# HGRN2 attention and a multiplicative FFN on one core: two early chunks in the later form, a fixed early order on VectorE, and a check in place of a clamp

## The chip, the core and the metric

One core of a Trainium2 chip runs the whole program: TensorE (PE) multiplies, VectorE (DVE), ScalarE (ACT) and GpSimd (POOL) do the elementwise work, and SyncE (SP) issues all the loads and stores as DMAs. Each engine takes its own list of instructions in order and waits on semaphores for the others. The metric is the device time of one execution in microseconds; lower is better. The time before is the median of 3 runs.

## What is computed

```
# attention: B,H,S,D = 4,8,768,48, all float32
f = 1 / (1 + exp(-f_logit))
for t in range(S):
    state = f[t][:, None] * state + outer(k[t], v[t])      # per batch and head, 48x48
    y[t] = q[t] @ state
x = y.transpose(0, 2, 1, 3).reshape(B * S, H * D)          # 3072 x 384
# FFN: w1, w2 384x1024; w3 1024x1024; w_out 1024x384, all float64
out = ((x @ w1) * (x @ w2)) @ w3 @ w_out                   # 3072 x 384, float32
```

## The kernel before

**Chunks.** The sequence is cut into 24 chunks of 128 steps (`NU`, six per batch). In a chunk the four pairs of heads lie side by side in 512 columns, two heads on partitions 0 to 47 and 64 to 111. ScalarE makes the gates by a sigmoid (L380); VectorE runs a forward scan over them (L388), a reciprocal (L398), a backward scan (L410), and multiplies to K (L418) and Q (L404). TensorE turns K (L455), forms K against Q, ScalarE copies the result (A), GpSimd cuts it to the causal half (L571), TensorE multiplies with v and adds what the state gives, and VectorE carries the state on.

**Two forms.** Chunks 0 to 3 (`u < NPE`) go in the *early form*: whole 128x128 products of K and Q (`pairs`, L431), `first_values` (L469, L475), `first_update` (L487), the state on VectorE (L687 to L690), and x^T by TensorE: `moved` multiplies with a permutation (L739), `settled` copies it into `xt` (L744). Chunks 4 to 23 go in the *later form*: 64-row tiles that run beside each other (L441, L548, L515, L534), a state in the middle of the chunk (`middle`, L619 to L624), a later gain (L683), and x^T by memory: `written` stores to DRAM (L731, two DMAs), `gathered` loads it back transposed (L734).

**FFN.** Four chunks make a block of 512 tokens, six blocks in all. Block 0 and a part of block 1 go by `part`: for each slice `jc` of 128 of the 1024 columns a product with w1, copied by ScalarE (L798), a product with w2, and VectorE's multiplication of the two (L803); block 0 takes the first four slices for two chunks at a time, the last four for all four. All other blocks go by seven products in place of eight (`seven`: TensorE L761, ScalarE's copies L864 and L892, VectorE L885 to L903), fed by sums of x^T (L831) and of the weights (L1253). w3 and w_out are folded into one matrix first: eight folds (L1221), copied by ScalarE (L1228), with sums of it (L1267). The down products use it (L997 to L1053). At most four banks of accumulators, the pool `f`, are open at once.

**Weights.** They arrive as float64, each number as two 32-bit words. `fetch` loads a piece (L1138), and each piece is made float32 by five instructions: ScalarE takes the magnitude of the high words (`magnitude`, L1157) and prepares the low words (`rest`, L1160); VectorE clamps the magnitude into the range whose exponent can be moved (L1163), shifts it by three bits (L1164), joins sign and low bits (`signed`, L1168) and adds (`joined`, L1174). There are 12 pieces of w1 and w2 (128x512), 4 of w_out (128x768) and 8 of w3 (128x1024). The landing buffers lie in one tile, `place`; a load waits until the piece that was there before is signed.

**Order.** `Plan` holds every step as a task with an engine, a cost in us, what it waits for, and a priority. `order()` takes again and again the task that can start first, lowest priority value among equals, and emits the instructions in that order; DMA slots (`lane`, 8), banks (`f`) and buffers (`ab`) are part of it. `need(u)` and the due times in `weights()` set the priorities. Until 35 us of planned time (`FULL`), holes in TensorE's list are filled with products of a constant (L268).

**The end.** `judge` looks at the ranges of the gates' products, `told` and `heard` send its result through DRAM, and before the last product of the last block (`final`, L1045) all engines read it: outside the safe range a general version of the attention runs instead of accepting the result.

Of the kernel before, what the change touches and what calls it, by code (L numbers as in the profile page):

```python
# [60 lines left out]
NPE = 4  # L61
# [7 lines left out]
W = C // 2  # L69
FULL = 35.0  # L70
FLOOR = 2.0**-60
# [3 lines left out]
class Plan:  # L75
# [16 lines left out]
    def add(self, eng, cost, emit, deps=(), prio=0.0, takes=(), frees=(), lag=0.2, slack=0.0):  # L92


        t = {
            "eng": eng, "cost": cost, "emit": emit, "deps": [d for d in deps if d is not None], "prio": prio,
            "takes": list(takes), "frees": list(frees), "lag": lag, "slack": slack, "at": None, "end": None, "no": len(self.tasks),
        }
        self.tasks.append(t)
        return t  # L100

    def order(self):
        free, done, left = {}, [], list(self.tasks)
        enders = {}
        for t in self.tasks:
            for f in t["frees"]:
                enders.setdefault(id(f), []).append(t)

        def after(t, ds):

            if any(d["end"] is None for d in ds):
                return None
            return max([0.0] + [d["end"] + (d["lag"] + t["slack"] if d["eng"] != t["eng"] else 0.0) for d in ds])

        def places(t, name):

            ends = [(after(t, enders[id(h)]) if h else 0.0, i) for i, h in enumerate(self.pools[name])]
            return [e for e in ends if e[0] is not None]

        def start(t):  # L120

            waits, at = list(t["deps"]), free.get(t["eng"], 0.0)
            for name in t["takes"]:
                if name in self.pools:
                    ends = places(t, name)
                    if not ends:
                        return None
                    at = max(at, min(ends)[0])
                    continue
                n, taken = self.slots[name]  # L130
                if len(taken) >= n:
                    waits += enders[id(taken[-n])]
            ready = after(t, waits)
            return None if ready is None else max(at, ready)

        while left:
            at, _, _, t = min(
                ((at, t["prio"], t["no"], t) for t in left if (at := start(t)) is not None), key=lambda x: x[:3]
            )
            t["at"], t["end"] = at, at + t["cost"]  # L140
            free[t["eng"]] = t["end"]
            for name in t["takes"]:
                if name in self.pools:
                    t["got"] = min(places(t, name))[1]
                    self.pools[name][t["got"]] = t
                else:
                    self.slots[name][1].append(t)
            left.remove(t)
            done.append(t)
        return sorted(done, key=lambda t: (t["at"], t["no"]))  # L150
# [3 lines left out]
def kernel(  # L154
# [19 lines left out]
    with tc.manual_schedule():  # L174
        outside = ranged(tc, q, k, f_logit, v, w1, w2, w3, w_out, out, ident, w12, wc, left)
        with tc.If(outside > 0, preferred_fallthrough_block=True, label="general"):
            general(tc, q, k, f_logit, v, leaf_mask, out, ident, w12, wc)
# [17 lines left out]
def ranged(ctx, tc, q, k, f_logit, v, w1, w2, w3, w_out, out, ident, w12, wc, left):  # L195
# [17 lines left out]
    back = keep.tile([R, NQ], F32, name="back")  # L213
    gate = [keep.tile([R, NQ + 1], F32, name=f"gate{i}") for i in range(2)]
    qs, ks, fs = ([keep.tile([R, NQ], F32, name=f"{nm}{i}") for i in range(n)] for nm, n in (("q", 3), ("k", 2), ("f", 2)))
    masked = [keep.tile([P, 2, HP, C], F32, name=f"A{i}") for i in range(2)]
    flat = [t.rearrange("p r h c -> p (r h c)") for t in masked]
# [105 lines left out]
    def need(u):  # L323
        return (0.0, 1.0, 2.0, 3.0)[u] if u < 4 else 60 + 14.5 * (u - 4)
# [4 lines left out]
    def moves(n, size, rate, emit, deps, prio, late=0.0):  # L329


        for j in range(n):
            i = plan.add("SP", 0.45, (lambda: None) if j else emit, [d] if j else deps, prio - j * 1e-3, takes=["lane"], lag=0.6)
            d = i
            t = plan.add("DMA", size / n / rate, lambda: None, [i], prio - j * 1e-3, lag=1.3 + late, frees=[i])
# [6 lines left out]
    def front(u):  # L342

        s, t = st[u], tk[u]
        n0 = need(u)

# [18 lines left out]

        t["lf"] = moves(2, 197, 250, load(fu, f_logit), free(2, "g"), n0 - 30)
        t["lk"] = moves(2, 197, 250, load(ku, k), free(2, "k"), n0 - 29.5)
        t["lq"] = moves(2, 197, 250, load(qu, q), free(3, "q"), n0 - 29)

        def load_v():  # L370
# [5 lines left out]
            n0 - (28.2, 28.2, 28.2, 29.6, 12)[min(u, NPE)],  # L376
# [29 lines left out]
        t["q"] = plan.add("DVE", 0.7, scale_q, [t["p"], t["lq"]] + past(u, 3, "v", "a"), n0 + 0.1)  # L406
# [13 lines left out]
        t["k"] = plan.add("DVE", 0.7, scale_k, [t["r"], t["lk"]] + past(u, 2, "a", "t"), n0)  # L420
# [209 lines left out]
    def rest(u):  # L630
# [13 lines left out]
        else:  # L644
            middle(u)
            more = u + 1 < NU
            after = tk[u + 1] if more else {}

            def visit():
# [4 lines left out]
                else:  # L654
                    s["pa"] = ps.tile([P, 2, NQ], F32, name="pa")
                    nc.tensor.transpose(out=s["pa"][:, 0, 0:R], in_=s["K"][:, 0:C], identity=ident[0:R, 0:R])
# [93 lines left out]
        else:  # L750
            t["z"] = moves(2, 197, 250, written, [t["y"]], n0 - 100)
            t["x"] = moves(1, 197, 250, gathered, [t["z"]] + before, n0 - 100)
# [13 lines left out]
    def ffn(n):  # L766
# [188 lines left out]
        if n == 0:  # L955
            part(0, 2, range(KH))
            part(2, 4, range(KH))
            part(0, 4, range(KH, KF))
# [150 lines left out]
    def fetch(loads_, a, prio, subs, deps=()):  # L1109
# [30 lines left out]
        ld = moves(1, total, 380, load, held, prio, max(0.0, 3.5 - 1.2 * load_no) if load_no < 4 * KM else 3.0)  # L1140
# [5 lines left out]
        def sub(c0, c1, dst, due, waits):  # L1146
# [9 lines left out]
            def magnitude():  # L1156
                nc.scalar.activation(m, hi.bitcast(F32), AF.Abs)  # L1157

# [3 lines left out]
            def shifted():  # L1162
                nc.vector.tensor_scalar(m, m, HIGH, LOW, ALU.min, ALU.max)  # L1163
                nc.vector.tensor_scalar(m.bitcast(U32), m.bitcast(U32), 3, None, ALU.logical_shift_left)  # L1164
# [12 lines left out]
            b = plan.add("ACT", 0.2 + 0.43 * w, magnitude, [ld] + past, due)  # L1177
            e = plan.add("ACT", 0.2 + 0.43 * w, rest, [ld], due)
            h = plan.add("DVE", 0.32 + 0.54 * w, shifted, [b], due)
            g = plan.add("DVE", 0.16 + 0.53 * w, signed, [e, b] + list(waits), due)  # L1180
# [13 lines left out]
    def weights():  # L1194
        due = {(0, 0): 5.0, (1, 0): 8.0, (0, 1): 24.0, (1, 1): 26.0}
        pieces.update({key: [] for key in due})
        for half in range(2):
            for which, w in enumerate((w1, w2)):
                for kc in range(KM):
# [3 lines left out]
                        [(slice(0, P), src)], 1, -26 + 9.5 * half + 0.5 * which + 0.1 * kc,  # L1203
                        [(0, KH * P, w12_part(which, kc, c0), due[which, half] + 0.1 * kc, [])],
                    )

        done = []
# [67 lines left out]

    def judge():
# [7 lines left out]
        good = work.tile([R, 1], F32, name="good")  # L1284
        nc.vector.tensor_scalar(low, low, RANGE, None, ALU.is_ge)
        nc.vector.tensor_tensor(good, low, nil, ALU.mult)
        where["good"] = good

    def told():
        where["all"] = dram.tile([R, 1], F32, name="good")  # L1290
        nc.sync.dma_start(where["all"], where["good"])

    def heard():
        row = work.tile([1, R], F32, name="row")
# [9 lines left out]
    for u in range(NU):  # L1304
        if u <= NPE:
            front(u)
        if u == NPE:
            turning(u)
            begin(u)
        if u >= NPE and u + 1 < NU:  # L1310
# [3 lines left out]
        if u == NPE - 1:  # L1314
            weights()
        if u == NU - 1:
            looked = plan.add("DVE", 1.0, judge, [tk[i]["y"] for i in range(NU)], -20)
            sent = moves(1, 0.4, 250, told, [looked], 0, 20.0)
            judged = plan.add("DVE", 0.2, decided, [moves(1, 0.4, 250, heard, [sent], 0, 20.0)], -20)
        if u % UB == UB - 1:  # L1320
            ffn(u // UB)
    ready_at = 0.0
# [8 lines left out]
    return blk[NB - 1]["outside"]  # L1331

# [336 lines left out]
```

## Time and profile before

| what | value |
|---|---|
| time, median of 3 runs | 477.67 us (477.29 to 477.99) |
| the profiled execution | 482.72 us, its span 481.0 us, mean granted TensorE clock 0.995 |
| VectorE / ScalarE / GpSimd busy | 362.8 us (75%) / 141.1 us (29%) / 62.5 us (13%) |
| bytes read / written | 40.67 MB / 8.65 MB |
| L388 and L410, the scans, 24 each | 29.6 us and 30.0 us |
| L418, L404: K and Q of a chunk, 112x512 | 738 ns, 684 ns |
| L1163 / L1164, 128x512, 12 each | 418 ns / 427 ns |
| L1168 / L1174, 128x512 pieces, 12 each | 758 ns / 690 ns |
| L1157 / L1160, 128x512, 12 each | 682 ns / 692 ns |
| load of a weight piece, 512 KB / 768 KB / 1024 KB, issue to landing | 9.7 us / 6.9 us / 4.7 us |
| yt<-ys / xt<-yt, issue to landing | 2.4 us / 2.9 us |

The span is that of one profiled execution, from the first to the last instruction; it took about 5 us more than the median of the runs. Lines such as L1163 are those of the kernel printed above. A duration in the profile includes an overlap with the next instruction of the same engine, so that the distance from start to start, which the timeline shows, is shorter.

### The profile page before, as it was taken

The numbers are of one execution on the slowest core, as the hardware profiler recorded it, in microseconds if no ns is written. First come the engines' busy times: TensorE is split into PE (matmuls) and PEld (weight loads), VectorE is DVE, ScalarE is ACT, GpSimd is POOL, SyncE is SP. The second block draws the span as 40 slices with busy tenths as digits, with TensorE's granted clock in tenths as the row PEclk, the third lists the DMA queues.
The fourth block names the chain that finished last, engine by engine and source line by source line (L and its number), as shares of the span: only waits on it lengthen the run. The fifth ranks groups of instructions, "written<-read, shape, count | busy, mean of one in ns | idle before, by whom it ended". The sixth has DMA issues, their size and how long they took to land.

```text
span 481.0 us, 11341 instructions
## 1 busy us (share of the span) xinstructions
PE 468.7 (97%) x4667; PEld 400.4 (83%) x4667; DVE 362.8 (75%) x706; ACT 141.1 (29%) x310; POOL 62.5 (13%) x88
## 2 busy tenths in 40 slices
PE   8899999999999899999999999999999999999996
PEld 7788644656799688889988889988899888889995
DVE  7999699999999689899999567357653667664541
ACT  4697456462313334432432110001100110110000
POOL 9300000013303133312422100000000000000000
PEclk9999999999999899999999999999999999999999
DMA  6899277743415566446531002000111000000011
GB/s 183 269 387 236 54 278 246 260 138 100 134 50 162 163 172 169 115 132 169 148 110 46 18 18 65 34 33 2 34 33 58 9 0 1 0 1 1 34 66 37
DMA packets 36618, 50.10 MB, mean 104 GB/s; under 512 B 4546, under 2 KB 26050, under 8 KB 35538
## 3 DMA queue, kind: packets, MB, share of 16 engines
q1 hardware_dynamic: 36562, 49.33, 33.6%
q8 instruction: 37, 0.61, 0.6%
q14 instruction: 19, 0.16, 0.1%
HBM read 40.67 MB, written 8.65 MB: 103 GB/s over the span
## 4 chain that ended last, share of the span: by engine, by line
PE 73%; DVE 13%; DMA 6%; POOL 3%; issue 2%; ACT 1%; SPq 1%; DVEq 0%; POOLq 0%; ACTq 0%
PE f L761 62%; DVE place L1168 2%; PE f L1221 2%; DMA place<-in_w_dram 2%; PE py L515 2%; DVE place L1174 2%; DMA place<-in_w_out_dram 2%; PE f L455 2%; PE pa L441 2%; PE pa L548 2%; PE py L534 1%; DMA f<-in_f_logit_dram 1%; SPq L1138 1%; POOL ab L306 1%; DVE place L1253 1%
## 5 line engine op out<-in xcount | busy, mean ns | idle before, releaser
L761 PE MATMUL f<-xt,w 128*128 128x256 f32 (+1 forms) x600 | 162.8, 401 | 3.2 <-ACT gate L380 2.0
L761 PEld LDWEIGHTS f<-xt,w 128*128 128x128 f32 x600 | 114.1, 192 | 29.5 <-issue 10.0
L761 PE MATMUL f<-place 128*128 128x192 f32 (+1 forms) x504 | 112.1, 349 | 0.1
L761 PEld LDWEIGHTS f<-place 128*128 128x128 f32 x504 | 87.7, 190 | 6.2 <-DVE place L1010 0.4
L571 POOL TENSOR_SCALAR_AFFINE_SELECT A<-A 64x512 f32<-64x512 f32 (+1 forms) x44 | 40.7, 925 | 120.3 <-ACT A L565 110.5
L1221 PE MATMUL f<-place 128*128 128x384 f32 x128 | 42.8, 489 | 0.2 <-DVE place L1174 0.2
L864 ACT COPY a<-f 128x256 f32<-128x256 f32 x36 | 13.4, 373 | 93.2 <-PE f L761 78.0
L1221 PEld LDWEIGHTS f<-place 128*128 128x128 f32 x128 | 23.8, 190 | 16.5 <-DVE place L1174 0.8
L761 PE MATMUL f<-xt,place 128*128 128x256 f32 x144 | 37.3, 382 | 0.0
L761 PE MATMUL f<-wc,ab 128*128 128x192 f32 x192 | 35.2, 327 | 0.0
L761 PEld LDWEIGHTS f<-wc,ab 128*128 128x128 f32 x192 | 32.0, 190 | 0.5
L410 DVE TENSOR_TENSOR_SCAN bwd<-gate,back 112x512 f32<-112x512 f32 x24 | 30.0, 1249 | 0.8
L388 DVE TENSOR_TENSOR_SCAN fwd<-gate,floor 112x512 f32<-112x512 f32 x24 | 29.6, 1233 | 1.1 <-ACT gate L380 0.3
L761 PEld LDWEIGHTS f<-xt,place 128*128 128x128 f32 x144 | 26.6, 189 | 3.3
L888 DVE TENSOR_TENSOR place<-f,a 128x256 f32<-128x256 f32 x36 | 15.3, 424 | 18.6 <-PE f L761 18.4
L1157 ACT ACTIVATE place<-place 128x512 f32<-128x512 f32 (+2 forms) x24 | 21.3, 886 | 8.2 <-DVE w L1174 3.8
L1160 ACT ACTIVATE place<-place 128x512 f32<-128x512 uint32 (+2 forms) x24 | 21.1, 885 | 5.1 <-DMA place<-in_w_out_dram 5.1
L674 POOL TENSOR_TENSOR G<-lasts,gate 112x4 f32<-112x4 f32 x20 | 11.1, 556 | 87.3 <-ACT lasts L393 55.2
L710 ACT ACTIVATE ys<-py 112x512 f32<-112x512 f32 x20 | 11.9, 596 | 35.6 <-PE py L534 34.6
L761 PE MATMUL f<-place,w 128*128 128x256 f32 x72 | 21.4, 379 | 0.0
L899 DVE TENSOR_TENSOR ab<-f,place 128x256 f32<-128x256 f32 x36 | 15.2, 423 | 6.2 <-PE f L761 5.3
L997 DVE TENSOR_TENSOR place<-ab 128x512 f32<-128x512 f32 x24 | 16.9, 702 | 3.5 <-PE f L761 3.5
(126 smaller groups left out, 642.9 us busy)
## 6 DMA issues: line engine op xcount, KB each, us to landing
place<-in_w_dram SPq DMA_DIRECT2D x8, 1024.0 KB, 4.7
place<-in_w_dram SPq DMA_DIRECT2D x12, 512.0 KB, 9.7
out_dram<-o SPq DMA_DIRECT2D x24, 192.0 KB, 1.9
q<-in_q_dram SPq DMA_DIRECT2D x46, 96.0 KB, 2.8
vt<-in_v_dram SPq DMA_DIRECT2D x23, 192.0 KB, 3.4
k<-in_k_dram SPq DMA_DIRECT2D x44, 96.0 KB, 2.3
f<-in_f_logit_dram SPq DMA_DIRECT2D x43, 96.0 KB, 2.5
yt<-ys SPq DMA_DIRECT2D x40, 96.0 KB, 2.4
```

What stands on the lines that cost most here:

```text
L388: nc.vector.tensor_tensor_scan(s["P"], gate[u % 2][:, 0:NQ], floor, 0.0, ALU.mult, ALU.max)
L410: nc.vector.tensor_tensor_scan(s["R"][:, ::-1], gate[u % 2][:, NQ:0:-1], back[:, ::-1], 0.0, ALU.mult, ALU.max)
L571: nc.gpsimd.affine_select(out=a, in_=a, pattern=pattern, compare_op=ALU.is_ge, fill=0.0, base=0, channel_multiplier=-1,)
L710: nc.scalar.activation(ys, py, AF.Copy, accum_out=ysum[:, u : u + 1])
L761: nc.tensor.matmul(out_, lhsT=lhs[i], rhs=rhs[i], start=start and i == 0, stop=i == len(lhs) - 1, skip_group_check=True,)
L864: nc.scalar.copy(q["a"], q["X"])
L888: nc.vector.tensor_tensor(ups["u3", k], q["Y"], q["a"], ALU.add)
L899: nc.vector.tensor_tensor(m if which else to(tok, half), q[bank_], m, ALU.add)
L997: nc.vector.tensor_tensor(abs_[j], x, y, op)
L1157: nc.scalar.activation(m, hi.bitcast(F32), AF.Abs)
L1160: nc.scalar.activation(lo.bitcast(F32), lo, AF.Copy, bias=2.0, scale=2.0**-51)
L1221: nc.tensor.matmul(w3s["p", jc], lhsT=w3s[jc][:, kc * P : kc * P + P], rhs=wos[:, kc], start=(kc == 0), stop=(kc == KF - 1),)
```

## The change

- **Forms.** `NPE` goes from 4 to 2: chunks 2 and 3 take the later form, x^T by memory included. They are not interleaved with the next chunk's products as later chunks are: a second constant, `SOLO`, keeps that for chunk 4 on.
- **VectorE's early order.** The string `EARLY` names the items in the order in which VectorE takes them after chunks 0 and 1: A, the first half of w1's columns; chunks 2 and 3; B, the first half of w2; C and D, the second halves of w1 and w2. Each item's first step waits for the last steps of the one before. The loads are asked for in the same order.
- **No clamp.** `magnitude` and the clamp go; the shift reads the high words directly, every second word of the landed piece, and drops the sign by itself.
- **A check.** `ranges` loads all weights once more after the last chunk, in 34 pieces of 512 numbers a partition, into the two buffers of A, and has ScalarE sum magnitudes (`AF.Abs`) and signs against a small bias (`AF.Sign`) of the high words; VectorE's `verdict` turns the sums into a yes or no that joins `judge`'s. For weights outside the range, `convert` makes them again with the clamp before the general version runs.
- **The plan's costs.** Every engine starts at 0.6; DMA rates and lags differ, transfers cost more in two stretches (`CROWDED`), DMA tasks queue by the time of their issue, and some loads have an earliest time (`since`, `AHEAD`).
- **Block 0** takes its last four slices in two halves of two chunks, like the first four. The last chunk's extra transpose (L656) goes.

```diff
-NPE = 4
+NPE = 2
+SOLO = 4
+WIDE = 2 * HP * C
+LOOK = WIDE // 2
+BEGIN = 0.6
+SURE = 2.0
+SURE_X = 1.0
+SURE_W = 2.0
+DUE = (5.0, 8.0, 24.0, 26.0)
+EARLY = "A23BCD"
+CROWDED = [(13.5, 19.5, 1.6), (33.0, 46.0, 1.3)]
+AHEAD = 22.0
...
-            t["at"], t["end"] = at, at + t["cost"]
+            t["at"], t["end"] = at, at + t["cost"] * slower(t, at)
...
         with tc.If(outside > 0, preferred_fallthrough_block=True, label="general"):
+            if w1.dtype != F32:
+                convert(tc, w1, w2, w3, w_out, w12, wc)
             general(tc, q, k, f_logit, v, leaf_mask, out, ident, w12, wc)
...
-    masked = [keep.tile([P, 2, HP, C], F32, name=f"A{i}") for i in range(2)]
-    flat = [t.rearrange("p r h c -> p (r h c)") for t in masked]
+    both = keep.tile([P, 2 * WIDE], F32, name="A")
+    flat = [both[:, i * WIDE : i * WIDE + WIDE] for i in range(2)]
+    masked = [t.rearrange("p (r h c) -> p r h c", r=2, h=HP) for t in flat]
...
-            more = u + 1 < NU
+            more = u + 1 < NU and u >= SOLO
...
-            part(0, 4, range(KH, KF))
+            part(0, 2, range(KH, KF))
+            part(2, 4, range(KH, KF))
...
-            def magnitude():
-                nc.scalar.activation(m, hi.bitcast(F32), AF.Abs)
-
             def rest():
                 nc.scalar.activation(lo.bitcast(F32), lo, AF.Copy, bias=2.0, scale=2.0**-51)
 
             def shifted():
-                nc.vector.tensor_scalar(m, m, HIGH, LOW, ALU.min, ALU.max)
-                nc.vector.tensor_scalar(m.bitcast(U32), m.bitcast(U32), 3, None, ALU.logical_shift_left)
+                nc.vector.tensor_scalar(m.bitcast(U32), hi, 3, None, ALU.logical_shift_left)
...
-            b = plan.add("ACT", 0.2 + 0.43 * w, magnitude, [ld] + past, due)
             e = plan.add("ACT", 0.2 + 0.43 * w, rest, [ld], due)
-            h = plan.add("DVE", 0.32 + 0.54 * w, shifted, [b], due)
-            g = plan.add("DVE", 0.16 + 0.53 * w, signed, [e, b] + list(waits), due)
+            h = plan.add("DVE", 0.16 + 0.27 * w, shifted, [ld] + past, due)
+            g = plan.add("DVE", 0.16 + 0.53 * w, signed, [e, h] + list(waits), due)
...
+    def ranges():
+
+        seen = [w[kc * P : kc * P + P] for w in (w1, w2) for kc in range(KM)] + [w3[jc] for jc in range(KF)]
+        seen.append(w_out.rearrange("(p a) c -> p (a c)", a=KF))
+        seen = [w[:, c : c + LOOK] for w in seen for c in range(0, w.shape[1], LOOK)]
+        n = len(seen)
+        sums_, counts, small = (spare[:, a : a + m] for a, m in ((0, n), (64, n), (128, 1)))
...
+        def load(i):
+            return lambda: nc.sync.dma_start(words[:, i % 2 * WIDE : (i % 2 + 1) * WIDE], seen[i].bitcast(U32))
+
+        def total(i):
+            a = hi[:, i % 2 * LOOK : (i % 2 + 1) * LOOK]
+            return lambda: nc.scalar.activation(a, a, AF.Abs, accum_out=sums_[:, i : i + 1])
+
+        def count(i):
+            a = hi[:, i % 2 * LOOK : (i % 2 + 1) * LOOK]
+            return lambda: nc.scalar.activation(a, a, AF.Sign, bias=small, accum_out=counts[:, i : i + 1])
+
+        for i in range(n):
+            ld = moves(1, LOOK, 400, load(i), last[:1] if i < 2 else last[i - 1 : i], 500 + i, SURE_W)
+            a = plan.add("ACT", 0.92, total(i), [ld], 500 + i)
+            last.append(plan.add("ACT", 0.95, count(i), [a], 500 + i))
+
+        def verdict():
+            nc.vector.tensor_scalar(sums_, sums_, LARGE, None, ALU.is_le)
+            nc.vector.tensor_scalar(counts, counts, LOOK - 0.5, None, ALU.is_ge)
+            nc.vector.tensor_tensor(sums_, sums_, counts, ALU.mult)
+            where["weights"] = small
+            nc.vector.tensor_reduce(out=small, in_=sums_, axis=AX.X, op=ALU.min)
+
+        return plan.add("DVE", 0.5, verdict, last, -20)
...
+    for item in EARLY:
+        if item in "ABCD":
+            half, which = divmod("ABCD".index(item), 2)
+            mine = pieces[which, half]
+            first[item], last[item] = [j["deps"][0] for j in mine], mine
+        else:
+            t = tk[int(item)]
+            first[item], last[item] = [t["p"]], [t["q"], t["k"]]
+    for a, b in zip("1" + EARLY, EARLY):
+        for t in first[b]:
+            t["deps"] += last[a] if a != "1" else [tk[1]["q"], tk[1]["k"]]
```

`convert`, which runs only where the general version does:

```
def convert(ctx, tc, w1, w2, w3, w_out, w12, wc):
...
    def single(src, dst):
...
        nc.scalar.activation(m, hi.bitcast(F32), AF.Abs)
        nc.scalar.activation(lo.bitcast(F32), lo, AF.Copy, bias=2.0, scale=2.0**-51)
        nc.vector.tensor_scalar(m, m, HIGH, LOW, ALU.min, ALU.max)
        nc.vector.tensor_scalar(m.bitcast(U32), m.bitcast(U32), 3, None, ALU.logical_shift_left)
...
```

## The prediction

> **What bounds the kernel now.** I read the page's busy shares and chain first, then the timelines of the engines where TensorE stops, then the windows there.
>
> ```profile
> PE 468.7 (97%) x4667; PEld 400.4 (83%) x4667; DVE 362.8 (75%) x706; ACT 141.1 (29%) x310; POOL 62.5 (13%) x88
> ...
> PE 73%; DVE 13%; DMA 6%; POOL 3%; issue 2%; ACT 1%; SPq 1%; DVEq 0%; POOLq 0%; ACTq 0%
> ```
>
> TensorE is busy for 97% of the span. Its last matmuls start at 474.75 us and take 1.46; 4.8 us of copy and store follow. So the end moves only by what TensorE idles, or by what it gets done before it is full. The chain puts 13% on VectorE, but where VectorE is fullest TensorE was full as well:
>
> ```profile
> 34.74 15.71 PE L761 MATMUL f<-xt,w 128*128 128x256 f32 x72
> 51.64 26.05 PE L761 MATMUL f<-xt,w 128*128 128x256 f32 x72 [1.20 <-ACT ab L798]
> 77.53 5.32 PE L1221 MATMUL f<-place 128*128 128x384 f32 x16
> 83.02 5.43 PE L1221 MATMUL f<-place 128*128 128x384 f32 x16 [0.17 <-DVE place L1174]
> ```
>
> From 34.74 on there is one pause of 1.2 us at 50.4, then the up products and the folds run end to end. The pause comes from ScalarE; a longer stop, at 159, comes from a landing of x^T:
>
> ```profile
> 50.45 0.88 ACT L1160 ACTIVATE place<-place 128x768 f32<-128x768 uint32 x1 [5.15 <-DMA place<-in_w_out_dram]
> ```
>
> ```profile
> 161.12 0.43 DVE L831 TENSOR_TENSOR place<-xt 128x256 f32<-128x256 f32 x1 [2.59 <-DMA xt<-yt]
> ```
>
> ```profile
> 159.00:160.00 1.00, 0.23 (x2) 0.00 (x0) 0.00 (x0) 0.74 (x3) 0.66 (x1) 1.00 0.41 121
> 160.00:161.00 1.00, 0.00 (x0) 0.00 (x0) 0.00 (x0) 0.26 (x1) 0.00 (x0) 1.00 0.39 115
> 161.00:162.00 1.00, 0.81 (x4) 0.76 (x5) 0.84 (x3) 0.00 (x0) 0.00 (x0) 0.96 0.91 261
> 162.00:163.00 1.00, 1.00 (x4) 0.82 (x3) 1.00 (x4) 0.00 (x0) 0.00 (x0) 0.50 0.89 233
> 163.00:164.00 1.00, 1.00 (x3) 0.76 (x3) 1.00 (x3) 0.37 (x1) 0.00 (x0) 0.50 0.37 105
> 164.00:165.00 1.00, 1.00 (x4) 0.79 (x3) 0.08 (x1) 0.00 (x0) 0.00 (x0) 0.50 0.48 144
> 165.00:166.00 1.00, 1.00 (x27) 0.59 (x29) 0.19 (x1) 0.00 (x0) 0.00 (x0) 0.84 0.88 217
> ```
>
> (After the stretch: its length, then PE, PEld, DVE, ACT, POOL busy, granted clock, DMA share, GB/s.) TensorE stands from 159.23 to 161.19 for chunk 7's x^T, and then its clock is at a half: 0.04 + 3 x 0.50 + 0.16 = 1.7 us more are lost.
>
> **No clamp.** A weight piece on VectorE, 128x512:
>
> ```profile
> 36.41 0.42 DVE L1163 TENSOR_SCALAR place<-place 128x512 f32<-128x512 f32 x1
> 36.86 0.43 DVE L1164 TENSOR_SCALAR place<-place 128x512 uint32<-128x512 uint32 x1
> 37.20 0.69 DVE L1168 SCALAR_TENSOR_TENSOR w<-place 128x512 uint32<-128x512 uint32 x1
> 37.92 0.69 DVE L1174 CUSTOM_DVE_ANT_0 w<-place,w 128x1024 uint16<-128x1024 uint16 x1
> ```
>
> From start to start these take 0.45 + 0.34 + 0.72 + 0.61 = 2.12 us. L1163 goes; by size that is 12 x 0.45 + 4 x 0.59 + 8 x 0.72 = 13.5 us of VectorE (starts at 59.14 and 73.51 for the larger ones). ScalarE loses 24 magnitudes, 8.2 + 3.7 + 9.4 = 21.3 us (L1157), and each piece loses one hand-over. The shift L1164 stays, but reads every second word of the landed buffer. No row has it so. Nearest row: the same operation in order, 0.43 (0.34 start to start); upper bound: L1168, which reads two spaced operands, 0.69 (0.72). A lower bound under 0.34 has no reason. L1168 takes what L418 takes on packed operands (0.69), so spacing cost nothing there: I take 0.34, a piece of 1.67. The Trainium skill (VectorE: DVE Perf Modes, Mode 2x_2P) gives the doubled rate to a one-source operation with source and target in SBUF and an even outer dimension, and asks no unit step; by it, too, the shift keeps 0.43.
>
> **VectorE's order, to the last piece of w2.** Chunk 1's Q ends at 14.11. w1's first half (A): 3 x 1.67 + 0.8 for a state = 19.9, but its last piece waits behind ScalarE's copies for chunk 1 (xt at 19.57 + 0.48, then 0.69): 21.0. Chunks 2 and 3: 14.21 to 24.16 before, less 1.2 of states = 8.8: 29.8. w2's first half (B): 5.0 + 2.1 of states (L621, L624, L683): 36.9. C: 5.0 + 0.7 + 4 products' L803 at 0.34 = 7.1: 44.0. D: 49.0. Before, the twelfth piece ended at 58.9.
>
> **TensorE's start.** In the new list four products that need A alone stand among chunks 2 and 3, done by about 35. Then it waits for B, 36.9; four products of 1.30 (6 matmuls at 0.217) and chunk 3's values (1.4): 43.5; four products on C from 44.0 to 49.2; the next needs x^T of chunks 2 and 3. The detour adds six DMAs to SP's queue (4 writes, 2 gathers, some 0.4 each); they stand behind the second w_out load, which waits until B's last piece is signed, about 35.6; before, that load took from 41.06 to 50.36, so it lands near 45; the writes behind it near 46, SP's 0.4 and the gather's 2.9 (median of xt<-yt): 49.5. Queued behind them are the last two w_out loads; VectorE reads these from 53 on, and a load took 4.7, so they may be asked for as late as 48. Before, the same twelve products were done and the next began at 51.64: 2.1 us won. The wait before 36.9 is as long as the one at 159, and if the clock halves as it did there, up to 1.7 us of it is lost through the chain. I take 1.6; ends: 2.9 (A not held by ScalarE) and -6.1 (rival 2).
> The later form itself takes 2.4 us of TensorE per chunk (155.33 to 157.75) against 5.6 (chunk 2's pieces from 18.30 to 29.29): 6.4 us less work, all of it in the start just counted. Its stop at 36.9 is what uses it up, so it is not counted again. Splitting eight 512-wide products into sixteen of 256 costs TensorE nothing (0.429 against 2 x 0.216 start to start), and VectorE 4 x 0.16 us.
>
> The rule of the Trainium skill (TensorE: Matmul & The Clock Gate, HAM oscillation) is that only pauses above about 3.4 us bring the clock down; here 2.0 us did. By the rule the start would win 2.1 instead of 1.6.
>
> **Folds.** 69 to 120 us: VectorE, 13 us lighter, is held by the folds it feeds (each third w3 row waits for a fold to free its buffer), so TensorE sets the pace. It wins the pauses of 0.34 and 0.29 that VectorE caused at 82 and 135: 0.7; ends 0 and 1.4.
>
> **The stop at 159.** In the new list chunk 7's values come before the first down product of block 0; before, after it (147.61). x^T of block 1 then lands some 20 us before it is read. 2.1 of stop and 1.7 of clock go: 3.8; ends 0 (another landing takes its place) and 4.2.
>
> **The check.** 34 loads of 512 KB and 68 ScalarE operations come after chunk 23. Bounds for one: below, L1157's 0.57 start to start; above, its 0.68 and 0.19 for reading the sum out (L710). I take the upper one: 59 us on an engine that is 10% busy from 276 on. Loads are hidden: DMA is near 0.1 there, and a load of 1024 KB took 4.7 us. They are listed across 20 seven-product groups (11 matmuls at 0.43 = 4.7 us) and 4 down products (7 x 1.3 = 9.1): 130 us, so the verdict stands near 400, 70 us ahead of the last product that waits for it. That cover gone, every us past 474 would count in full. Queued behind one operation's wait for its load are TensorE's bank copies (L864, L892); behind SP's waits, output stores and x^T gathers that are not due. I take 0.5 us; ends 0 and 7.5 (rival 1).
>
> **Sum.** 1.6 + 0.7 + 3.8 - 0.5 = 5.6 us. The profiled execution took 482.72 (span 481.0, 1.7 around it), so 477.1 for such a one; it stood 5.05 above the median of the runs, 477.67. Forecast: 477.67 - 5.6 = 472.1.
>
> **Rivals.**
> 1. ScalarE's check holds TensorE's copies (slower). 38 copies lie in the 130 us; ScalarE is taken 59/130 = 45% of it, and a copy that meets an operation waits half of 0.87: 38 x 0.45 x 0.44 = 7.5 us. For it: the engine keeps its order, and the copy that frees a product's first bank has only 0.86 us of other matmuls over it. Against: the operations stand in holes of 2 us (ScalarE's idle before L864 is 78 us in 24 waits). 472.1 + 7.0 = 479.1; slower from 0.16 us a copy on. 0.12.
> 2. The detour by memory is late: the second w_out load lands at 50.4 as before, then 2.4 + 0.4 + 2.9: the thirteenth product at 56.1, 4.4 later than before, and 1.7 of clock: 472.1 + 1.6 + 6.1 = 479.8. For it: DMA is full from 20 to 45. Against: the weights are asked for 6 us earlier. 0.07.
> 3. The spaced shift runs at 0.72: 12 x 0.38 = 4.6 us until D's end, which TensorE waits for: 476.7. 0.08.
> 4. The stop at 159 only moves: 475.9. 0.10.
>
> **How the numbers follow.** The forecast has 0.63, with 469.5 to 474.5 as its own range (the ends of its terms other than the rivals'). Best ends together: 2.9 + 1.4 + 4.2 = 8.5, 469.2; TensorE's pauses under 0.25 us sum to 17.5 us (starts against the median of their form, over the whole timeline), and if an eighth went too, 467.0, the low end. The high end, 479.3, takes in rivals 1, 3 and 4. What a measurement of this kernel can tell from no change is 0.2%, 476.7 to 478.6. Faster: the forecast, rival 4 and a part of 3: 0.76; same 0.08; slower, rivals 1 and 2 in the main, 0.16.
>
> **What would show it.** Twelve w1/w2 pieces done near 49; the shift's row at 0.43; the up products unbroken from about 50; no stop near 159 and no 0.5 in the clock there; ScalarE at about 45% in the stretch after chunk 23 with TensorE at 100%; last matmul near 470.5. Wrong if TensorE shows a stop over 2 us after 50, or if pauses come behind L864 after 276.

## The result, and the profile after

The changed kernel takes 481.76 us (median of 9 runs, 480.47 to 485.46); the kernel before took 477.67 us beside it (median of 9). The ratio is 1.0078, with a 95% interval of 1.0056 to 1.0101: the change made the kernel slower by about 4 us, where 5.6 us less were forecast. A second comparison (a_after, median of 4 runs) gave 482.14 against 478.11 us, 1.0091 [1.0055, 1.0127].

The page of the profiled execution (482.74 us, span 480.9) has these busy shares, and this share of each engine in the chain that ended last:

```profile
PE 466.5 (97%) x4850; PEld 406.3 (84%) x4850; DVE 352.9 (73%) x695; ACT 173.2 (36%) x420; POOL 61.0 (13%) x90
...
PE 93%; DMA 2%; DVE 1%; SPq 1%; issue 0%; ACT 0%; POOL 0%; POOLq 0%; ACTq 0%; DVEq 0%
```

VectorE is lighter by 9.9 us, as meant, and has left the chain (13% to 1%). But TensorE's end stays where it was in the profile of before, 476.41 against 476.21 us. TensorE's timeline shows where the work fell behind (start, length, operation, how many):

```profile
15.33 0.60 PE L488 MATMUL py<-ident,K 112*128 112x112 f32 x4
20.94 2.93 PE L769 MATMUL f<-ys,ab 112*128 112x128 f32 x12 [5.00 <-ACT ys L740]
...
32.95 2.77 PE L791 MATMUL f<-xt,w 128*128 128x256 f32 x12
...
44.98 0.70 PE L791 MATMUL f<-xt,w 128*128 128x256 f32 x2 [1.20 <-DVE w L1201]
...
46.98 28.76 PE L791 MATMUL f<-xt,w 128*128 128x256 f32 x132
75.58 5.32 PE L1250 MATMUL f<-place 128*128 128x384 f32 x16
```

It stands for 5.0 us at 15.9, does five up products (30 records, six each) by 45.7, and is full only from 46.98. The kernel before had twelve done at 50.4. The folds do begin at 75.58, earlier than before, but with only 162 of block 0's 192 units of up products done (a unit is a record of 256 columns, 0.216 us; a 512-wide record counts as two). Why TensorE stood is in ScalarE's list:

```profile
14.29 0.69 ACT L1188 ACTIVATE place<-place 128x512 f32<-128x512 uint32 x1 [1.25 <-DMA place<-in_w_dram]
19.68 0.63 ACT L413 ACTIVATE gate<-ab 112x512 f32<-112x512 f32 x1 [4.70 <-DMA ab<-in_f_logit_dram]
20.21 0.58 ACT L740 ACTIVATE ys<-f 112x512 f32<-112x512 f32 x1
...
23.90 0.48 ACT L774 COPY xt<-f 128x384 f32<-128x384 f32 x1 [1.14 <-PE f L769]
24.27 0.67 ACT L1188 ACTIVATE place<-place 128x512 f32<-128x512 uint32 x1
```

Chunk 2's gate (L413, at 19.68) stands in the list ahead of chunk 0's output copy (L740), which TensorE waits for, and ahead of the low halves of w1's second and third piece (L1188), which VectorE waits for. Its input landed after 19.5 us. SP's timeline tells why; the changed kernel asked for three weight loads of 512 KB in front of it:

```profile
7.75 1.38 SPq L1169 DMA_DIRECT2D place<-in_w_dram  x3
9.23 1.92 SPq L387 DMA_DIRECT2D ab<-in_f_logit_dram  x2
```

From issue to landing that input took some 10 us. In the kernel before the two early gate inputs of chunks 2 and 3 were asked for first, at 7.3 and 10.6 us, the weights from 14.3 on, and a load of that kind took 2.6 us (median of four before 22 us). VectorE's list shows the cost for the weights:

```profile
19.17 0.43 DVE L1191 TENSOR_SCALAR place<-place 128x512 uint32<-128x512 uint32 x1 [1.98 <-DMA place<-in_w_dram]
21.48 0.69 DVE L1195 SCALAR_TENSOR_TENSOR w<-place 128x512 uint32<-128x512 uint32 x1 [1.88 <-ACT place L1188]
...
25.01 0.36 DVE L719 TENSOR_TENSOR S<-py,S 112x192 f32<-112x192 f32 x1 [2.11 <-ACT place L1188]
...
27.07 1.22 DVE L421 TENSOR_TENSOR_SCAN fwd<-gate,floor 112x512 f32<-112x512 f32 x1
```

w1's first half, 5 us of work, takes VectorE from 14.1 to 27.07, with 6.8 us of waits in it: 2.5 for landings of the weights, 4.3 for ScalarE. A part of the latter is TensorE's clock, which was at a half from 18.9 to 25.7 us: chunk 0's x^T (L769) took 2.93 us, against 1.61 at full clock in run e1 below, and the low half of the third piece (L1188 at 24.27) stands behind its copy (L774).

To compare starts I use one number S: the start of the first fold, plus 0.216 us for each unit of block 0's up products still to do then. It says when the work up to the folds would be done, if nothing stopped it any more. The "rest" is the end of TensorE's last matmul less S.

| profile | S | last matmul ends | rest |
|---|---|---|---|
| before, as shown with the prediction | 77.5 | 476.2 | 398.7 |
| before, once more (b_before) | 76.1 | 472.7 | 396.6 |
| changed | 82.1 | 476.4 | 394.4 |
| changed, once more (a_after) | 81.3 | 475.6 | 394.4 |

So the change loses 5 to 6 us up to the folds and wins about 2 behind them, against the second profile of before (478.81 us), which stands at the median. Against the first it loses 4.6 and wins 4.3.

### The profile page after: what moved, and what is told of

The parts are those of the page before. It is cut to its first block, busy times and chain, and to the rows that moved or that the text cites. A ratio compares the mean times of both kernels' runs of the same rounds, so it can differ in the third digit from the quotient of the medians.

```text
span 480.9 us, 11858 instructions
## 1 busy us (share of the span) xinstructions
PE 466.5 (97%) x4850; PEld 406.3 (84%) x4850; DVE 352.9 (73%) x695; ACT 173.2 (36%) x420; POOL 61.0 (13%) x90
## 4 chain that ended last, share of the span: by engine, by line
PE 93%; DMA 2%; DVE 1%; SPq 1%; issue 0%; ACT 0%; POOL 0%; POOLq 0%; ACTq 0%; DVEq 0%
PE f L791 71%; PE f L1250 9%; PE py L548 3%; PE pa L474 2%; DMA ab<-in_f_logit_dram 2%; PE pa L581 2%; PE py L567 2%; PE f L488 2%; PE f L769 1%; SPq L387 1%; PE f L294 1%; DVE w L1195 0%; DVE w L1201 0%; SPq L1169 0%; PE f L508 0%
## 5 line engine op out<-in xcount | busy, mean ns | idle before, releaser
L791 PE MATMUL f<-xt,w 128*128 128x256 f32 x648 | 163.3, 381 | 1.2 <-DVE w L1201 1.2
L791 PEld LDWEIGHTS f<-xt,w 128*128 128x128 f32 x648 | 121.3, 190 | 18.1 <-DVE w L1201 1.6
L604 POOL TENSOR_SCALAR_AFFINE_SELECT A<-A 64x512 f32<-64x512 f32 (+1 forms) x46 | 38.8, 842 | 115.7 <-ACT A L598 108.7
L1325 ACT ACTIVATE A<-A,back 128x512 f32<-128x512 f32 x34 | 26.3, 772 | 0.8
L1321 ACT ACTIVATE A<-A 128x512 f32<-128x512 f32 x34 | 23.0, 676 | 5.7 <-DMA A<-in_w_dram 5.7
L1188 ACT ACTIVATE place<-place 128x512 f32<-128x512 uint32 (+2 forms) x24 | 21.2, 888 | 7.1 <-DMA place<-in_w_dram 7.1
L740 ACT ACTIVATE ys<-py 112x512 f32<-112x512 f32 x22 | 13.1, 597 | 27.3 <-PE py L567 27.0
L413 ACT ACTIVATE gate<-f 112x512 f32<-112x512 f32 x22 | 13.9, 632 | 23.8 <-DVE bwd L443 11.3
L791 PE MATMUL f<-place,w 128*128 128x256 f32 x72 | 21.5, 380 | 0.0
```

Of the source, the lines that this page charges most:

```text
L413: nc.scalar.activation(gate[u % 2][:, 0:NQ], fu, AF.Sigmoid)
L604: nc.gpsimd.affine_select(out=a, in_=a, pattern=pattern, compare_op=ALU.is_ge, fill=0.0, base=0, channel_multiplier=-1,)
L791: nc.tensor.matmul(out_, lhsT=lhs[i], rhs=rhs[i], start=start and i == 0, stop=i == len(lhs) - 1, skip_group_check=True,)
L1188: nc.scalar.activation(lo.bitcast(F32), lo, AF.Copy, bias=2.0, scale=2.0**-51)
L1321: return lambda: nc.scalar.activation(a, a, AF.Abs, accum_out=sums_[:, i : i + 1])
L1325: return lambda: nc.scalar.activation(a, a, AF.Sign, bias=small, accum_out=counts[:, i : i + 1])
```

## The experiments

All times are medians; each ratio is to the kernel before, run on the same chip beside it, and can differ a little from the quotient of the two medians. S and the timelines are those of one profiled execution of each kernel.

### The profile of before, once more (b_before)

No edit.

> The kernel before, profiled once more, since its profiled execution of 482.7 us stood 5.05 us above its median. Theory: most executions of the kernel before do not have the stop of 2.1 us near 159 us with the 1.7 us of half clock behind it; a profile of 477 to 478.5 us shows TensorE without either. Rival: the stop is in every execution, and the 5 us lie somewhere else, in the first 50 us or spread over the small pauses; then a profile of 478 us shows the stop at 159 as before.

Measured: 478.78 us against 478.79, ratio 1.001 [0.9995, 1.0026]. The timeline of TensorE has no pause at 50 us, and the stop near 157 is there, without the half clock behind it (windows: stretch, length, busy PE, PEld, DVE, ACT, POOL, granted clock, DMA share, GB/s):

```profile
34.79 41.48 PE L761 MATMUL f<-xt,w 128*128 128x256 f32 x144
76.11 4.36 PE L1221 MATMUL f<-place 128*128 128x384 f32 x13
```

```profile
158.00:159.00 1.00, 0.00 (x0) 0.00 (x0) 0.00 (x0) 0.60 (x2) 0.05 (x1) 1.00 0.38 104
159.00:160.00 1.00, 0.64 (x3) 0.62 (x4) 0.69 (x2) 0.00 (x0) 0.00 (x0) 1.00 0.71 212
160.00:161.00 1.00, 1.00 (x7) 0.87 (x6) 0.98 (x4) 0.07 (x1) 0.00 (x0) 1.00 0.89 246
```

Neither theory held whole: the stop (1.96 us over the usual distance of two records) is in both profiles; the pause at 50 (1.36) and the 1.7 us of half clock are only in the execution that the prediction was costed on. In an execution at the median the stop was worth about 2 us, not 3.8.

### The gate of chunk 2, believed later (e1)

```diff
-        t["lf"] = moves(2, 197, 300, load(fu, f_logit), free(2, "g"), ask[0], since=since)
+        t["lf"] = moves(2, 197, 300, load(fu, f_logit), free(2, "g"), ask[0], 6.0 if u == 2 else 0.0, since=since)
```

> The changed kernel, with one number in the planner altered: it believes that the gate input of chunk 2 lands 6 us later than it did. The loads and VectorE's fixed order stay; ScalarE's order moves chunk 2's gate behind the low halves of w1's first half and chunk 0's output copy. Theory (that gate stood at the head of ScalarE's queue from 14.98 to 19.68 us, waiting for a load that was asked for behind three weight loads, and the weights and TensorE stood behind it): VectorE's scan of chunk 2 begins near 21.5 us instead of 27.1, TensorE resumes near 18.5 instead of 20.9, and the time falls by 3 to 5 us, to 477 to 479. Rival (the weights land late in any order, and ScalarE's order is no matter): the same within 1 us, 481 to 482.5.

Measured: 478.92 us, ratio 1.0007 [0.9984, 1.003]. S is 78.0 where the changed kernel has 81.3 and 82.1. TensorE and VectorE in its timelines:

```profile
16.95 1.61 PE L769 MATMUL f<-ys,ab 112*128 112x128 f32 x12 [1.13 <-ACT ys L740]
...
25.99 2.76 PE L791 MATMUL f<-xt,w 128*128 128x256 f32 x12
```

```profile
20.46 1.21 DVE L421 TENSOR_TENSOR_SCAN fwd<-gate,floor 112x512 f32<-112x512 f32 x1
```

Up to the first up products the loads are asked for in the same order as in the changed kernel; what differs is ScalarE's order, and what the planner derives from it. (The landings themselves vary: the third weight piece is shifted at 17.84 us here, at 19.17 in the changed kernel.) The scan comes 6.6 us earlier, the first up product 7.0, TensorE stands for 1.13 us instead of 5.0, its clock stays full, and some 3 us of the loss are gone. The gate at the head of ScalarE's queue, with the half clock that followed the stop, is so shown as the larger part of the loss. The 1.9 us of S that are left against b_before are not traced to their end; a pause of 1.13 us before 47.63, in which TensorE waits for VectorE's weights, is among them.

### Chunks 2 and 3 first (e2)

```diff
-EARLY = "A23BCD"
+EARLY = "23ABCD"
```

> The changed kernel with VectorE's early order (and the order in which the loads are asked for) set to chunks 2 and 3 first and all weight pieces behind them, as the kernel before had it. The later form, the detour by memory and the missing clamp stay. Theory (w1's first half in front of chunks 2 and 3 makes the lost start): no wait of ScalarE for a gate input, w1's last piece near 30 us, w2's near 36, the third near 41, the fourth near 46; up products without the pauses up to 47 us; 475.5 to 478.5 us. Rival (the later form and the detour by memory lose the start, whatever the order): no faster than 480.

Measured: 476.64 us, ratio 0.9957 [0.9941, 0.9973]: faster than the kernel before by 2 us, with the later form, the missing clamp and the check all in place. S is 76.0, the rest 394.1.

```profile
32.43 1.46 PE L791 MATMUL f<-xt,w 128*128 128x256 f32 x6
33.82 1.00 PE L548 MATMUL py<-A,place 64*64 64x64 f32 x32
...
35.19 10.20 PE L791 MATMUL f<-xt,w 128*128 128x256 f32 x46
45.71 22.71 PE L791 MATMUL f<-xt,w 128*128 128x256 f32 x104 [0.32 <-DVE w L1201]
```

The order of the change, weights in front of chunks, is what lost the start: with the chunks first S is 5 to 6 us lower. Yet S is no better than before's 76.1, though the setup has 6.4 us of TensorE less: the first product comes 2.4 us earlier, and chunk 3's values (1.4) and a pause for the next weights (0.48 over the usual distance, before 45.71) use most of it up.

### The input of chunk 2 asked for first (e8)

```diff
+        if u == 2:
+            ask = [x - 3.0 for x in ask]
```

> The changed kernel with the loads of chunk 2 (f_logit, k, q) asked for ahead of w1's first half; VectorE's fixed order stays. Theory (it is the late landing of chunk 2's gate input, behind three weight loads of 512 KB, that ScalarE's queue stands on): ScalarE's gate of chunk 2 by 15 us, VectorE's scan of chunk 2 near 20 to 21.5 us instead of 26 to 27, folds 3 to 5 us earlier than in the changed kernel, ratio to the kernel before 0.998 to 1.003. Rival (weights ahead of chunks lose the start however the loads are asked for): ratio over 1.005.

Measured: 481.29 us, ratio 1.006 [1.0037, 1.0082]: the rival. S is 80.7. Chunk 2's gate is computed at 11.55, as expected, but now chunk 3's gate blocks ScalarE, chunk 0's x^T copy (L776) behind it:

```profile
21.54 0.63 ACT L415 ACTIVATE gate<-ab 112x512 f32<-112x512 f32 x1 [3.00 <-DMA ab<-in_f_logit_dram]
22.07 0.46 ACT L776 COPY xt<-f 128x384 f32<-128x384 f32 x1
```

and VectorE's scan of chunk 2, its input long there, comes only at 24.46 (20 to 21.5 expected, 27.07 in the changed kernel), since the fixed order puts it behind w1's pieces, whose loads are now later. TensorE then runs at half clock from 25.5 to 32.3 us, which takes its part of what was won. So asking for one input earlier isn't enough: another instruction that waits is now in front. The first theory, that only chunk 2's late input mattered, was too narrow.

### Chunk 3 alone behind w1's first half (e4, then e9)

```diff
-EARLY = "A23BCD"
+EARLY = "2A3BCD"
```

> The changed kernel with VectorE's early order (and that of the loads) chunk 2, then w1's first half, then chunk 3 and the rest. Theory (what lost the start was chunk 2's gate input asked for behind three weight loads, not chunk 3's place): no ScalarE wait for a gate input over 1 us, w1's first half done near 26 to 28 us, up products from 28 us; as fast as with both chunks first, or up to 1.5 us faster, a ratio to the kernel before of 0.992 to 0.997. Rival (any weight piece ahead of a chunk loses the start): ratio over 1.0.

Measured: 478.85 us, ratio 1.0017 [0.9998, 1.0036]: on the rival's side, and not told from no change. The up products start at 27.36, 7 us before those of the kernel before, but S is 76.3 all the same. TensorE stops again, at 44.7, and the cause is another gate, that of chunk 4, for which ScalarE stands 4.46 us with chunk 3's output copy behind it:

```profile
42.38 0.63 ACT L413 ACTIVATE gate<-f 112x512 f32<-112x512 f32 x1 [4.46 <-DMA f<-in_f_logit_dram]
42.92 0.58 ACT L740 ACTIVATE ys<-py 112x512 f32<-112x512 f32 x1
```

```profile
45.99 22.71 PE L791 MATMUL f<-xt,w 128*128 128x256 f32 x104 [1.29 <-DVE w L1201]
```

To see whether that is the same mechanism, the planner was told of late gates there too, with the same order:

```diff
-EARLY = "A23BCD"
+EARLY = "2A3BCD"
...
-        t["lf"] = moves(2, 197, 300, load(fu, f_logit), free(2, "g"), ask[0], since=since)
+        t["lf"] = moves(2, 197, 300, load(fu, f_logit), free(2, "g"), ask[0], {3: 1.5, 4: 4.0}.get(u, 0.0), since=since)
```

> The changed kernel with the early order chunk 2, w1's first half, chunk 3 and the rest, and the planner told that the gate inputs of chunks 3 and 4 land 1.5 and 4 us later. In the run without that, ScalarE stood at chunk 4's gate from 37.9 to 42.4 us, chunk 3's output copy and VectorE's state behind it, and TensorE for 1.46 us at 44.3. Theory (the same mechanism a second time): the wait for chunk 4's gate goes, chunk 3's output copy comes near 41.1 us, the pause at 44.3 shrinks to 0.5 us or less, and the time falls by 1 to 2 us, ratio to the kernel before 0.993 to 0.999. Rival (TensorE runs dry there for want of x^T from memory): the pause stays, ratio 1.000 to 1.003.

Measured: 477.3 us (475.8 to 480.71), ratio 0.9994 [0.9973, 1.0014]. In the profile the pause shrinks from 1.46 to 0.41 us over the usual distance, and S is 74.7, the best of all:

```profile
44.13 22.71 PE L791 MATMUL f<-xt,w 128*128 128x256 f32 x104 [0.25 <-DVE w L1201]
```

The mechanism is seen, but the medians don't settle the gain: the intervals of this run and of e4 overlap, and this kernel's runs scatter more.

### The clamp back, with the chunks first (e5)

```diff
-EARLY = "A23BCD"
+EARLY = "23ABCD"
...
+            def magnitude():
+                nc.scalar.activation(m, hi.bitcast(F32), AF.Abs)
...
             def shifted():
-                nc.vector.tensor_scalar(m.bitcast(U32), hi, 3, None, ALU.logical_shift_left)
+                nc.vector.tensor_scalar(m, m, HIGH, LOW, ALU.min, ALU.max)
+                nc.vector.tensor_scalar(m.bitcast(U32), m.bitcast(U32), 3, None, ALU.logical_shift_left)
...
```

> The changed kernel with chunks 2 and 3 first in VectorE's order, and the clamp back: ScalarE's magnitude, VectorE's minimum and maximum, and the shift of packed words, with the planner's costs of the kernel before. The check stays. Theory (with the chunks first, VectorE's pieces set the pace of the up products, so the 12 operations of 0.45 us count in part): w2's last piece near 56 us instead of 50.6, pauses of 2 to 5 us in the up products, ratio to the kernel before 1.000 to 1.006 where the kernel without the clamp had 0.9957. Rival (TensorE is full, and VectorE's 13 us are hidden): ratio 0.994 to 0.998.

Measured: 482.03 us, ratio 1.0083 [1.0053, 1.0112], a little beyond the theory's range; S is 82.0, 6 us later than without the clamp.

```profile
33.35 10.76 PE L791 MATMUL f<-xt,w 128*128 128x256 f32 x48
48.36 32.51 PE L791 MATMUL f<-xt,w 128*128 128x256 f32 x138 [4.25 <-DVE place L1195]
```

With chunks 2 and 3 in the later form, 48 units stand on TensorE's list for the first two weight quarters and the x^T of chunks 0 and 1; the next need the third quarter, and VectorE sets the time. But not all of the 6 us is the clamp's own work: behind the stop of 4.25 us TensorE does its products at half clock from 48.36 to 53.4 us, which loses another 2.5.

### The clamp out of the kernel before (e7)

```diff
-            def magnitude():
-                nc.scalar.activation(m, hi.bitcast(F32), AF.Abs)
...
             def shifted():
-                nc.vector.tensor_scalar(m, m, HIGH, LOW, ALU.min, ALU.max)
-                nc.vector.tensor_scalar(m.bitcast(U32), m.bitcast(U32), 3, None, ALU.logical_shift_left)
+                nc.vector.tensor_scalar(m.bitcast(U32), hi, 3, None, ALU.logical_shift_left)
...
```

> The kernel before, with the clamp alone taken out: ScalarE's magnitude and VectorE's minimum and maximum go, and the shift reads the landed words; no check of the ranges is added, and chunks 2 and 3 keep their earlier form. Theory (with x^T by TensorE, TensorE is full from 34.8 us whatever VectorE does, so VectorE's 13 us win next to nothing at the start; they can only bring later chunks forward): w2's last piece near 52 us instead of 58.9, the up products from 34.8 us without a pause, as before; the folds begin near 76 us, as before; the time the same within 0.3%, or down by at most the 2 us of the stop near 157 if chunk 7 comes forward. Rival (VectorE's pieces bound the kernel before): 472 to 475 us, ratio under 0.994.

Measured: 477.63 us, ratio 0.9984 [0.9967, 1.0002]. S is 77.2, no better than 76.1; the rest is 393.5, 3.1 us less. Chunk 7's values come at 125.4 us (145.9 with the clamp), and the stop near 157 is gone. So with x^T by TensorE the clamp costs nothing at the start, and what its absence wins in this profile lies behind the start, where later chunks come forward. The interval just reaches no change.

### The earlier form back, with the chunks first (e6)

```diff
-NPE = 2
+NPE = 4
...
-EARLY = "A23BCD"
+EARLY = "23ABCD"
```

> The changed kernel with chunks 2 and 3 first in VectorE's order, and in the earlier form (x^T by TensorE, no detour by memory). Theory (the first up products wait for VectorE's pieces, so the 6.4 us of TensorE that the later form saves lie in idle time or behind the start, and at most a part counts): the first up product near 34 us, ratio to the kernel before 0.995 to 1.002. Rival (all TensorE time counts): 4 us or more above the kernel with the later form, ratio over 1.004.

Measured: 476.8 us, ratio 0.9966 [0.9948, 0.9984], not told from 0.9957 with the later form. First product at 35.07, S 76.5. The later form's 6.4 us of TensorE are worth half a microsecond of S here, and nothing that the medians can tell. The timelines suggest why: with the early form the up products run from 35.07 to the folds without a pause, as the x^T of chunks 2 and 3 is there; the later form begins 2.6 us earlier and then stops for chunk 3's values and for weights.

### The check left out (e3)

```diff
-        if wide:
-            nc.vector.tensor_tensor(good, good, where["weights"], ALU.mult)
...
-            weighed = [ranges()] if wide else []
+            weighed = []
```

> The changed kernel without the check of the weights' ranges: the 34 loads, the 68 ScalarE operations and the verdict are left out, and the rest of the decision stays. Theory (the check costs only the 0.5 us that the feed-forward matmuls of 256 columns took longer after 276 us, 0.2168 against 0.2160 us from start to start): 480.5 to 481.5 us, not told from the changed kernel. Rival (the check's copies held up TensorE's banks, or its loads held up x^T): 477 to 479 us.

Measured: 481.14 us, ratio 1.0052 [1.0033, 1.0072], where the changed kernel has 1.0078 and 1.0091. The profile tells the check's own price from the rest: TensorE's last 1000 distances from the start of one matmul record to the next (553 from a record of 256 columns, 447 from one of 192, none over 0.41 us) sum to 191.99 us in both profiles of before, in this run and in e7, the four without the check, and to 192.57 in both of the changed kernel: 0.58 us. (In the other eight profiles with the check it is 192.56 to 192.82.) What this profile wins beyond that lies in the start (S 79.6): the gate's input came earlier, TensorE stood for 3.27 us, not 5.0, and its clock was at a half for 3.4 us, not 6.8. The window 300 to 350 us of the changed kernel shows how the check was carried:

```profile
300.00:350.00 50.00, 50.00 (x253) 45.51 (x253) 29.70 (x70) 24.44 (x66) 0.00 (x0) 1.00 0.46 154
```

ScalarE (fourth) is taken 49% there, where before it was 10%, and TensorE stays at 50.00 of 50.

### w_out later, with the chunks first (e10)

```diff
-EARLY = "A23BCD"
+EARLY = "23ABCD"
...
-        ld = moves(1, total, 400, load, held, prio, SURE)
+        ld = moves(1, total, 400, load, held, prio, SURE, since=43.0 if load_no >= 4 * KM else 0.0)
```

> The changed kernel with chunks 2 and 3 first, and the w_out loads held back to 43 us in the planner, so that they are asked for behind chunk 3's x^T. In the run without that, chunk 3's values ended at 35.3 us, its write was asked for at 36.6 to 38.2 and landed only at 44.06, and x^T was gathered from there. Theory (the detour's transfers are slow since they stand beside weight loads): x^T of chunk 3 lands before 44 us, the pause of 0.48 us at 45 goes, and the time falls by 0.3 to 1 us, ratio 0.993 to 0.9955. Rival (w_out's pieces come late and hold the folds): ratio 0.997 or more.

Measured: 476.4 us, ratio 0.9962 [0.9944, 0.9979], not told from 476.64 and 0.9957. x^T of chunk 3 was asked for at 40.85 instead of 44.06 us, so the detour by memory was slowed by w_out's loads, but the pause stays, since the next products on TensorE's list need the weights:

```profile
45.65 25.30 PE L791 MATMUL f<-xt,w 128*128 128x256 f32 x116 [0.32 <-DVE w L1201]
```

## Why the prediction was wrong

**The step that failed: "w1's first half (A): 3 x 1.67 + 0.8 for a state = 19.9, but its last piece waits behind ScalarE's copies for chunk 1 ...: 21.0".** The pieces cost what was said: from 53.18 to 54.84 a piece takes 1.66 us from start to start, and the shift of every second word takes 0.42, 0.33 to the next start, as the packed one did. But A ended at 27.07, because the step took inputs as landed. It counted the detour's DMAs in SP's queue and not those that the new order moved ahead of chunk 2's gate input; and it didn't look who stands behind the gate on ScalarE. Some 1.3 us of it is the half clock behind the stop (x^T of chunk 0 in 2.93 us against 1.61 in e1), which the step had not either. The error of 6.1 us went on: chunks 2 and 3 ended at 35.2 (forecast 29.8), B at 44.8 (36.9), C at 51.1 (44.0), D at 56.5 (49.0). The start was forecast to win 1.6 us and lost 4.6 by S against the profile that the prediction was costed on (82.1 against 77.5), and 6.0 against the one near the median (76.1). None of the rivals had this mechanism; rival 2 put the danger in the x^T by memory, which did come later than forecast (asked for from 48.9 us) but found TensorE busy with other products from 46.98 to 75.58.

**A step beside it, "6.4 us less work, all of it in the start just counted".** That TensorE's saved work wins little was right, but for more than its reason: even with the chunks first (e2, e6) the later form gives S 76.0 against 76.5. What bounds that start is when weights and x^T are there: in e2 the stop before 45.71 ends with a weight piece, and in e6 there is none.

**No clamp.** VectorE's saving was sized well by piece. Where it pays was not seen: nothing at the start of the kernel before (e7), and 6 us where the later form leaves TensorE nothing else to do (e5), 2.5 of them by the half clock behind the stop.

**The stop at 159: 3.8 forecast.** The mechanism was right: chunk 7's values come at 130.4 us instead of 147.6, and no stop over 0.35 us is left between 47 us and the end. The size held against the profile that it was costed on: folds, stop and check together were forecast at 0.7 + 3.8 - 0.5 = 4.0, and the rest fell by 4.3. It was not that of the median: the second profile has 2.0 us there and not the half clock, and against it the rest fell by 2.2 us, with the check's 0.6 in it. What moved the products is not settled to one part: the stop is gone with the clamp out of the old plan (e7), and also with the clamp back in the new plan (e5).

**The sum against the median.** The profiled execution stood 5.05 us above the median, and the sum took winnings from it that the second profile, near the median, did not have to give: 1.4 us at 50, 1.7 of half clock. By S and rest of that profile, 477.67 + 6.0 - 2.2 = 481.5; measured 481.76. (That is the difference of two profiles and no independent test.)

**Folds and check.** The two VectorE pauses in the folds are gone, as said, but the one of 0.34 at 83 is not in the second profile of before either. The check was forecast at 0.5 us and costs 0.58; rival 1, 7.5 us, is out.

**The signs.** The up products unbroken from 50, no stop near 159, no half clock there and ScalarE at 49% beside a full TensorE all came true, and neither sign of being wrong appeared: both looked behind 50 us. What failed stands ahead of it: twelve pieces done at 56.5 instead of 49.

**Faster than both.** The changed kernel with chunks 2 and 3 first (e2) has the lowest ratio, 0.9957 [0.9941, 0.9973]; e6 and e10 are not told from it, so neither the form of the two chunks nor holding back w_out makes a difference that these runs can tell.

## What to carry to other kernels

When an order is changed, the loads change places too: for each moved step write down when its input lands by the new queue, and what stands behind the waiting instruction on each engine that takes its list in order. A planner that believes a load early puts its consumer in front of work that is ready; telling it a later landing brought back 3 us with the loads asked for in the same order. And before a stop is booked as a gain, see in a second profile, near the median, that it is there.

## What the hardware showed

The half clock behind short stops comes and goes. The same stop of 1.96 us was followed by a clock of 0.50 for over 3 us in one execution of the kernel before, and by 1.00 in another. In the changed kernel the clock fell 3 us into the stop of 5.0 us, and came back only 4.8 us after the work resumed at 20.94:

```profile
18.00:19.00 1.00, 0.00 (x0) 0.00 (x0) 0.00 (x0) 0.00 (x0) 0.00 (x0) 0.94 0.73 191
19.00:20.00 1.00, 0.00 (x0) 0.00 (x0) 0.43 (x1) 0.32 (x1) 0.00 (x0) 0.50 0.14 46
...
24.00:25.00 1.00, 1.00 (x17) 0.91 (x16) 0.00 (x0) 1.00 (x3) 0.00 (x0) 0.50 1.00 274
25.00:26.00 1.00, 1.00 (x4) 0.85 (x5) 0.89 (x3) 0.46 (x1) 0.00 (x0) 0.65 0.85 250
```

There x^T of chunk 0 took 2.93 us instead of the 1.61 of e1. In e8 two stops of 1.56 and 1.01 us, 1.6 us of work between them, brought 0.50 from 25.5 to 32.3. The half clock lasted 3.41 us in the first profile of before and 3.42 in e3, and 6.82 or 6.83 in both of the changed kernel, in e5 and in e8: one length, once or twice. In before it began at 161.92 and in e3 at 19.82, each 0.7 us after TensorE had resumed. The other eight profiles have none. The Trainium skill (TensorE: Matmul & The Clock Gate, Part 1: The HAM clock gate) says that the gate watches a window of about 3.4 us that runs freely. The lengths agree with it. That could make one stop fall into a window or across two; where a window begins no run here shows by itself, and stops under 3.4 us did bring the clock down.

The other surprise is the queue: a gate input of 2 x 96 KB behind three loads of 512 KB took some 10 us to land, and 2.6 us ahead of them. The Trainium skill (DMA: Bandwidth & Descriptors, Queues, rings and completion order) says that each DMA engine takes the descriptors of a queue's ring in their order there, which agrees with it.
